# Attention and feed-forward kernel: first query halves on two hardware queues ahead of the other keys, first bursts on the first half, score pieces in unit pairs

## Chip, cores, metric

One core of one Trainium2 chip. The metric is device time in microseconds, the median of several executions. Runs are told apart by state (fast or slow); all timed runs below are fast ones. The one single run, of the experiment with delayed software loads, has the state unknown, and only its trace is used.

## The reference

Grouped-query attention (8 batches, 16 query heads, 4 key heads, 384 positions, 64 elements per head), then a feed-forward layer with a squared ReLU:

```python
scores = (1/sqrt(64)) * q @ k.T          # per batch and head; 4 query heads share a key head
attn   = softmax(scores)
x      = (attn @ v) -> [3072, 1024]
out    = (max(x @ w_in, 0) ** 2) @ w_out # w_in 1024x2048, w_out 2048x1024
```

## The kernel before

A recorder collects operations with what they read and write, and turns them into semaphore waits. It also keeps a clock per engine with a cost for each operation. A loop, the list scheduler, uses these clocks to choose what TensorE does next. The loads of batch 0, with the key of head 0 (`k0`) first:

```python
def first_loads():
    for g0, g1 in ((0, 1), (1, HKV)):              # k0, then the other keys: both on sync
        R.add("sync", lambda e, ...: e.dma_start(k_f32[...g0:g1...], k[0, g0:g1]...),
              writes=[("k_f32", g) ...], dma=f"kf{g0}", cost=0.4 if g1 == 1 else 1.6, issue=0.4)
    for n in range(2):                             # the two q halves of key head 0: both on scalar
        R.add("scalar", lambda e, n=n: e.dma_start(q_f32[:, 2*n:2*n+2, :], q[0, 2*n:2*n+2]...),
              writes=[("q_f32", n)], dma=f"qf{n}", cost=0.8, issue=0.4)
# ... cut: GpSimd's own (software) loads and casts, in its program order:
load_q(0, 4, 8); ...; load_v(0); load_q(0, 8, 12); load_q(0, 12, 16); load_w_in(0)
dup_k(0, 1, 2)        # cast of key head 1, waits for the other keys
load_k(1); dup_k(0, 2, 4); aug_v(0, "gpsimd"); load_q(1, 0, 8); ...
```

Batch 0 is scored in small bursts. Each burst is two or four matmuls, and one exponential on ScalarE reads its result. A unit is one key head's block of 128 keys; units 0 to 2 belong to head 0. Elements 0 to 383 of a unit's row need the first q half, the rest the second.

```python
for group in ((0,), (1, 2), (3, 4), (5, 6), (7,), (8, 9), (10, 11)):
    if len(group) == 2 and group[1] < NU - 1:
        smalls += [[(u, 0, 512)] for u in group] + [[(u, 512, 256) for u in group]]
    else:
        smalls += [[(u, c0, 384)] for c0 in (0, 384) for u in group]
turn_q = [(0, 0, "a"), (0, 0, "c")]   # transposes of the first and second q half
turn_q += [(b, g, w) for b in range(2) for g in range(HKV) for w in "kq" if (b, g) != (0, 0)]
# ... cut: in the scheduling loop
if turn_q and (b == 0 or pairs < 6 or x_done[0] == 8):
    cand.append((..., 3.5 * b + 1, "turn"))        # priority 1; a score burst of batch 0 has 0
```

The softmax here doesn't subtract the row's maximum and nothing guards it: scores larger than these inputs give would overflow.

## Time and profile before

| | |
|---|---|
| median | 430.89 us (3 runs, 430.09 to 431.02) |
| span of the profiled run | 428.1 us |
| TensorE busy | 423.2 us, 99% |
| ScalarE busy | 194.9 us, 46% |
| half-clock window in the profile | 8.08 to 11.49 us |

TensorE has 99% of the span, and the chain of waits is TensorE's for 98%. Only what delays TensorE's start can be removed without removing work. The prediction shows the lines. Here is the trace's transfer view of the kernel before from 3.8 to 5.0 us. Its columns are the queue row, the packets, the megabytes moved, and the time those packets took as a share of 16 engines' time. Row q1 is the sync queue, q10 the scalar queue, q0 GpSimd's software loads.

```profile
DMA packets 565, 0.32 MB, mean 266 GB/s; under 512 B 270, under 2 KB 565, under 8 KB 565
q0 software_dynamic: 242, 0.09, 67.6%
q10 hardware_dynamic: 233, 0.17, 41.6%
q1 hardware_dynamic: 90, 0.06, 15.2%
```

### The profile page before, as it was taken

What the parts mean: (1) busy time and instruction counts of PE and PEld (TensorE: products, weight loads), DVE (VectorE), ACT (ScalarE), POOL (GpSimd) and SP (SyncE); (2) the same over time, 40 slices, a digit from 0 to 9 for tenths busy, and PEclk for the clock granted to TensorE, in tenths of its full rate; (3) what the DMA queues carried; (4) which work ended last, traced back from release to release, by engine and by line L of the source; (5) the groups of instructions that cost most, each with busy time, mean ns of one, the idle gap of its engine ahead of it and who ended that gap; (6) DMA issues with size and microseconds to landing.
All of it is one profiled execution on the core that took longest, in us unless ns stands there. A gap on an engine that the chain in (4) does not pass through costs nothing.

```text
span 428.1 us, 7844 instructions
## 1 busy us (share of the span) xinstructions
PE 423.2 (99%) x3467; PEld 232.2 (54%) x3467; DVE 158.8 (37%) x334; ACT 194.9 (46%) x194; POOL 55.1 (13%) x67
## 2 busy tenths in 40 slices
PE   7999999999999999999999999999999999999997
PEld 5565554565445654456554465645564465446544
DVE  2674432254223542325432253523342144214412
ACT  6947740557545675446765459550230033003300
POOL 8680011413040022004000000000000000000000
PEclk8999999999999999999999999999999999999999
DMA  9999999999599179369647410032001100110012
GB/s 180 193 198 204 187 195 190 236 152 130 90 188 166 20 133 141 98 145 145 64 80 140 89 45 18 16 92 81 37 2 49 73 26 2 49 73 26 1 66 83
DMA packets 95347, 43.90 MB, mean 103 GB/s; under 512 B 75728, under 2 KB 89296, under 8 KB 95312
## 3 DMA queue, kind: packets, MB, share of 16 engines
q0 software_dynamic: 36544, 17.44, 32.4%
q1 hardware_dynamic: 58224, 25.57, 28.0%
q8 instruction: 27, 0.44, 0.4%
q10 hardware_dynamic: 544, 0.39, 0.3%
q14 instruction: 8, 0.07, 0.1%
HBM read 35.65 MB, written 12.58 MB: 113 GB/s over the span
## 4 chain that ended last, share of the span: by engine, by line
PE 98%; DMA 1%; ACT 0%; DVE 0%; ACTq 0%; issue 0%
PE ps L431 40%; PE ps L480 39%; PE ps L374 9%; PE ps L349 7%; PE ps L328 1%; DMA q_f<-in_q_dram 1%; PE ps L302 1%; PE ps L407 0%; PE ps L286 0%; ACT expT L338 0%; DVE o_sb L389 0%; ACT q_st L551 0%; ACTq L218 0%; DVE y_sb L489 0%; DVE rinv L383 0%
## 5 line engine op out<-in xcount | busy, mean ns | idle before, releaser
L431 PE MATMUL ps<-xT,w_in_sb 128*128 128x384 bf16 x1024 | 175.0, 326 | 0.0
L480 PE MATMUL ps<-w_out_sb,h2T 128*128 128x512 bf16 (+2 forms) x784 | 172.0, 375 | 0.0
L359 ACT ACTIVATE expT<-ps 128x3072 bf16<-128x3072 f32 x42 | 114.4, 2725 | 57.7 <-PE ps L349 57.1
L431 PEld LDWEIGHTS ps<-xT,w_in_sb 128*128 128x128 bf16 x1024 | 96.8, 98 | 69.2 <-issue 6.4
L441 ACT ACTIVATE h2T<-hr 128x384 bf16<-128x384 f32 x128 | 64.3, 520 | 148.8 <-DVE hr L439 148.7
L480 PEld LDWEIGHTS ps<-w_out_sb,h2T 128*128 128x128 bf16 x784 | 73.8, 98 | 87.6 <-issue 5.4
L439 DVE TENSOR_SCALAR hr<-ps 128x384 f32<-128x384 f32 x128 | 71.1, 557 | 104.8 <-PE ps L431 104.8
L489 DVE COPY y_sb<-ps 128x512 f32<-128x512 f32 (+2 forms) x49 | 33.4, 681 | 127.4 <-PE ps L480 127.4
L374 PEld LDWEIGHTS ps<-v_aug,expT 128*128 128x128 bf16 x1152 | 39.8, 97 | 6.6 <-DVE o_sb L389 0.7
L374 PE MATMUL ps<-v_aug,expT 128*128 128x65 bf16 x1152 | 41.6, 193 | 0.1
L389 DVE TENSOR_TENSOR o_sb<-ps,rinv 128x384 bf16<-128x384 f32 x64 | 35.7, 558 | 2.2
L349 PE MATMUL ps<-qT,kT 64*128 64x512 bf16 (+1 forms) x336 | 34.6, 325 | 0.0
L349 PEld LDWEIGHTS ps<-qT,kT 64*128 64x128 bf16 x336 | 13.0, 94 | 20.7 <-issue 5.4
L383 DVE RECIPROCAL rinv<-ps 128x6 f32<-128x6 f32 x64 | 12.2, 190 | 24.1 <-PE ps L374 24.0
L338 ACT ACTIVATE expT<-ps 128x1024 bf16<-128x1024 f32 (+1 forms) x20 | 17.2, 941 | 1.7 <-PE ps L328 1.5
L263 POOL COPY v_aug<-v_st 128x768 bf16<-128x768 bf16 x8 | 6.7, 832 | 87.0 <-PE ps L374 71.9
L258 POOL COPY k_dup<-k_st 128x1536 bf16<-128x1536 bf16 x7 | 10.3, 1467 | 36.7 <-DMA k_st<-in_k_dram 36.7
L231 POOL DMA_DIRECT2D q_st<-in_q_dram x17 | 14.9, 888 | 0.9 <-POOLq L726 0.8
L205 POOL DMA_DIRECT2D k_st<-in_k_dram x7 | 5.3, 762 | 39.6 <-DMA qT<-q_st 39.6
L328 PE MATMUL ps<-qT,kT 64*128 64x384 bf16 (+2 forms) x48 | 8.0, 360 | 0.3 <-DVE qT L309 0.2
L241 POOL DMA_DIRECT2D w_in_sb<-in_moe_w_in_dram x8 | 7.1, 897 | 0.0
L224 POOL DMA_DIRECT2D v_st<-in_v_dram x8 | 6.3, 792 | 0.1
(26 smaller groups left out, 44.5 us busy)
## 6 DMA issues: line engine op xcount, KB each, us to landing
out_dram<-y_sb SPq DMA_DIRECT2D x47, 256.0 KB, 2.0
q_st<-in_q_dram POOLq DMA_DIRECT2D x14, 384.0 KB, 9.1
w_in_sb<-in_moe_w_in_dram POOLq DMA_DIRECT2D x8, 512.0 KB, 12.1
w_out_sb<-in_moe_w_out_dram POOLq DMA_DIRECT2D x4, 1024.0 KB, 27.0
v_st<-in_v_dram POOLq DMA_DIRECT2D x8, 192.0 KB, 10.6
k_st<-in_k_dram POOLq DMA_DIRECT2D x7, 192.0 KB, 4.3
q_st<-in_q_dram POOLq DMA_DIRECT2D x3, 192.0 KB, 5.2
xT<-o_sb SPq DMA_TRANSPOSE x28, 4.3
```

The lines of the kernel that those rows point to most:

```text
L231: R.add("gpsimd", lambda g: g.dma_start(q_st[st][:, h0:h1, :], q[b, h0:h1].rearrange("h (p j) d -> p h (j d)", j=NJ)), writes=[("q_st", st ...
L328: mm = pe.matmul(ps[:, base + x, m * wide:(m + 1) * wide], kT[b % 2][64 * x:64 * x + 64, u, :], q_cols(b, u // NJ, x, c0, c0 + wide))
L338: R.add("scalar", lambda e: e.activation(dst, src, AF.Exp, scale=0.125), reads=keys, writes=[("expT", (b * NU + u) % NEX, t) for u, _, _ i ...
L349: m = pe.matmul(flat[:, k0 * HC + c0:k0 * HC + c1], kT[b % 2][64 * x:64 * x + 64, u + k0, :], q_cols(b, (u + k0) // NJ, x, c0, c1))
L359: R.add("scalar", lambda e: e.activation(dst, src, AF.Exp, scale=0.125), reads=keys, writes=[("expT", (n + m) % NEX, t) for m in range(2) ...
L374: m = pe.matmul(po[:, f - 6 * s2, 0:D + 1], w, v_aug[b % 2][:, g * NJ + j, 0:D + 1], start=(j == 0), stop=(j == NJ - 1))
L389: R.add("vector", lambda e: e.tensor_tensor(dst, srcv, rbv, ALU.mult), reads=[("bank", i), ("rinv", r)], writes=[("o_sb", o, s2)], cost=0.48)
L431: m = pe.matmul(bank(i)[:, 0:S], w_in_sb[:, kc, c * 128:(c + 1) * 128], xT[b % NXT][:, kc, :], start=(kc == 0), stop=(kc == NKC - 1))
L439: R.add("vector", lambda e: e.tensor_scalar_max(hr[r][:, :], bank(i)[:, 0:S], 0.0), reads=[("bank", i)], writes=[("hr", r)], cost=0.48)
L441: R.add("scalar", lambda e: e.activation(h2T[b % 2][:, c, :], hr[r][:, :], AF.Square), reads=[("hr", r)], writes=[("h2T", b % 2, c)], cost ...
L480: m = pe.matmul(bank(i)[:, 0:n], h2T[b % 2][:, c, i3 * 128:(i3 + 1) * 128], w_out_sb[:, c, c0:c1], start=(c == 0), stop=(c == NFC - 1))
L489: R.add("vector", lambda e: e.tensor_copy(ysl, bank(i)[:, 0:n]), reads=[("bank", i)], writes=[("y", yb)], cost=0.08 + n / 960)
```

## The change

The intent is to have TensorE score as soon as the first q half is there. The second q half moves from the scalar to the sync queue, ahead of the other keys. The second half's transposes may not stand ahead of the first burst. The bursts are grouped so that the first two need the first q half alone.

```diff
-        for g0, g1 in ((0, 1), (1, HKV)):
-            R.add("sync", lambda e, g0=g0, g1=g1: e.dma_start(
+        def keys(g0, g1):
+            R.add("sync", lambda e: e.dma_start(
   ...
-                ..., cost=0.4 if g1 == 1 else 1.6, issue=0.4)
-        for n in range(2):
-            R.add("scalar", lambda e, n=n: e.dma_start(
+                ..., cost=0.4 if g1 == 1 else 1.1, issue=0.4)
+        def queries(n, eng):
+            R.add(eng, lambda e: e.dma_start(
   ...
+        keys(0, 1)
+        queries(0, "scalar")
+        queries(1, "sync")
+        keys(1, HKV)
   ...
-    for group in ((0,), (1, 2), (3, 4), (5, 6), (7,), (8, 9), (10, 11)):
-        if len(group) == 2 and group[1] < NU - 1:
+    for group in ((0, 1), (2, 3), (4, 5), (6, 7), (8, 9), (10, 11)):
+        if 0 < group[0] < NU - 2:
   ...
-        if turn_q and (b == 0 or pairs < 6 or x_done[0] == 8):
+        if turn_q and (b == 0 or pairs < 6 or x_done[0] == 8) and (sc_q[0] != (0, 0) or w in "ka"):
```

More of the change, by code (lines that the diff above doesn't have):

```diff
@@ L210, in first_loads @@
     def first_loads():
-        for g0, g1 in ((0, 1), (1, HKV)):
-            R.add("sync", lambda e, g0=g0, g1=g1: e.dma_start(
+        def keys(g0, g1):
+            R.add("sync", lambda e: e.dma_start(
                 k_f32[:, g0 * NJ:g1 * NJ, :].rearrange("p (g j) d -> p g (j d)", j=NJ),
                 k[0, g0:g1].rearrange("g (p j) d -> p g (j d)", j=NJ)),
-                writes=[("k_f32", g) for g in range(g0, g1)], dma=f"kf{g0}", cost=0.4 if g1 == 1 else 1.6, issue=0.4)
-        for n in range(2):
-            R.add("scalar", lambda e, n=n: e.dma_start(
+                writes=[("k_f32", g) for g in range(g0, g1)], dma=f"kf{g0}", cost=0.4 if g1 == 1 else 1.1, issue=0.4)
+        def queries(n, eng):
+            R.add(eng, lambda e: e.dma_start(
                 q_f32[:, 2 * n:2 * n + 2, :], q[0, 2 * n:2 * n + 2].rearrange("h (p j) d -> p h (j d)", j=NJ)),
                 writes=[("q_f32", n)], dma=f"qf{n}", cost=0.8, issue=0.4)
+        keys(0, 1)
+        queries(0, "scalar")
+        queries(1, "sync")
+        keys(1, HKV)
     def load_v(b):
```

## The prediction

> **What bounds the kernel now.** I read the page first. The busy line and the chain that ended last say that TensorE is the bound almost from end to end:
>
> ```profile
> span 428.1 us, 7844 instructions
> PE 423.2 (99%) x3467; PEld 232.2 (54%) x3467; DVE 158.8 (37%) x334; ACT 194.9 (46%) x194; POOL 55.1 (13%) x67
> PE 98%; DMA 1%; ACT 0%; DVE 0%; ACTq 0%; issue 0%
> ```
>
> The reader is to see how little is not TensorE: 2% of 428.1 us is some 8 us. The change touches only the first loads and the scores of batch 0, so all it can remove is part of that. I then asked the trace for the chain of waits in its first 31 us, to see where those microseconds lie:
>
> ```profile
> 0.73 0.46 ACTq L218
> 1.23 4.05 DMA q_f<-in_q_dram
> 5.30 0.52 ACT q_st L551
> 5.82 0.14 issue
> 5.96 0.33 PE ps L302 x3
> 6.29 0.29 PE ps L328 x2
> 6.59 0.82 ACT expT L338
> 7.46 0.39 PE ps L328 x2
> 7.85 0.52 PE ps L302 x6
> ```
>
> (Columns: start, duration, what.) The head of the program hangs on the second q load: it is issued at 1.23 us and lands at 5.28, ScalarE casts it (L551), TensorE transposes it (L302), the first score burst (L328) follows, its exponential (L338) frees the banks, and from 7.46 us on every piece of the chain is TensorE, apart from 0.9 us near 23 us. So before 7.46 us lies the removable time.
>
> The timeline of that stretch shows why the first score burst waited for the second q load though it reads only the first half:
>
> ```profile
> 4.96 0.36 DVE L309 COPY qT<-ps 128x384 bf16<-128x384 bf16 x1 [0.38 <-PE ps L302]
> 5.30 0.51 ACT L551 CAST q_st<-q_f 128x384 bf16<-128x384 f32 x1 [0.97 <-DMA q_f<-in_q_dram]
> 5.96 0.33 PE L302 MATMUL ps<-ident,q_st 128*128 128x128 bf16 x3 [1.03 <-ACT q_st L551]
> 6.22 0.34 PE L328 MATMUL ps<-qT,kT 64*128 64x384 bf16 x2
> 6.32 0.36 DVE L309 COPY qT<-ps 128x384 bf16<-128x384 bf16 x1 [1.00 <-PE ps L302]
> 6.59 4.35 ACT L338 ACTIVATE expT<-ps 128x768 bf16<-128x768 f32 x5 [0.78 <-PE ps L328]
> 11.54 7.03 ACT L338 ACTIVATE expT<-ps 128x1024 bf16<-128x1024 f32 x8 [0.59 <-PE ps L328]
> 18.72 5.91 ACT L338 ACTIVATE expT<-ps 128x1024 bf16<-128x1024 f32 x7 [0.16 <-PE ps L328]
> ```
>
> The transposed first half is ready at 4.96 + 0.36 = 5.32 us. But TensorE runs in program order, and the transposes of the second half stand ahead of the burst: TensorE idles 1.03 us for the cast, transposes, and only then scores. The last three lines show the second thing: from 6.59 to 24.63 us ScalarE has only 0.59 + 0.16 us of idle time, so the 20 exponentials of batch 0 and TensorE run neck and neck there. No transfer holds TensorE up after 6 us: in the list of waits of the TensorE rows over the whole span, none names a DMA.
>
> **What the Trainium skill says.** Four places bear on this.
> - "DMA: Bandwidth & Descriptors", section "Issuing engines are not separate DMA queues": transfers from SP, ACT and GpSimd share the same 16 engines, and issuing from several saves only issue time. The trace agrees: from 3.2 to 3.8 us the two hardware rows together moved 355 GB/s, and from 5.0 us, when the software row has the engines, it is about 180 GB/s. So moving a load to the other queue buys no bandwidth; only its order can matter.
> - Same page, "Queues, rings and completion order": each engine takes turns between rows packet by packet. The trace agrees only in part: from 2.2 to 3.2 us row q10 moved 0.19 MB and q1 0.10, from 3.2 to 3.8 us q1 0.17 and q10 0.04, from 3.8 to 4.4 us q10 0.14 and q1 0.06. That is rather one transfer after the other in order of issue. I reckon with that order.
> - "TensorE: Matmul & The Clock Gate", "What's actually happening": the array runs at half rate until a free-running window of 3413 ns was busy, and falls back after an idle one. The trace agrees: the granted clock is 1.00 until about 8.1 us, 0.50 until 11.5, then 1.00, so one such window after the sparse stretch from 4.7 to 8.1 us.
> - "ScalarE: Activation LUTs", "What ACT_TABLE_LOAD costs": an activation with immediate scale costs 186 ns + 0.833 ns per element. That gives 826 ns for 768 and 1039 for 1024; the groups by form show 816 and 1025 ns. So the new grouping, if it keeps the counts, keeps ScalarE's total.
>
> **The change part by part.**
>
> *Loads.* The bytes stay: one key group 96 KB, two q halves of 192 KB, the other keys 288 KB. Issue order was k0 and q-first (both 0.73 us), other keys (about 1.13), q-second (1.23). Now q-second is second on the sync queue, ahead of the other keys. In order of issue it takes the place that the other keys had: they had moved about 0.23 MB by 3.8 us (row q1's 0.33 MB less k0's 0.10). The 0.20 MB of q-second should be through at about 3.7 us. The first q half had moved by 3.2 us and landed at 3.8, so 0.6 us for the completion: q-second lands at about 4.3 us instead of 5.28, an estimate. ScalarE casts the first half from 3.82 to 4.33, so the second cast follows at 4.35 to 4.9 us instead of 5.30 to 5.81. The other keys come last: at 4.4 us 0.76 of the 0.79 MB had moved before, and the total is the same, so they land at about 5.3 us instead of 5.1. GpSimd casts them at 6.09 us without having waited, after issuing four software loads, so it loses nothing.
>
> *First bursts.* The new condition lets the first burst go before the second half's transposes, and with units (0, 1) as the first group two bursts in a row read only the first half. Burst 0 starts when the first half's copy is done: 5.32 + 0.05 us (the second burst began 0.05 us after its copy ended at 6.68) = 5.37 instead of 6.21. Its exponential starts 0.38 us later, as before (6.59 - 6.21): 5.75 instead of 6.59, so 0.84 us sooner. The first half itself (land, cast, transpose, copy) doesn't move, so it is the new head. The second half's transposes come behind burst 1, at about 5.9 us; their copy is done at about 6.7, and the exponential of burst 1 runs until 5.75 + 2 x 0.82 = 7.4, so burst 2 isn't late for ScalarE.
>
> *Grouping.* Counted from the loops: before 2 + 3 + 3 + 3 + 2 + 3 + 4 = 20 bursts, now 4 + 4 x 3 + 4 = 20; eight of 768 elements and twelve of 1024 in both. No instruction and no time is added on ScalarE or TensorE. What moves: the pair (2, 3) straddles two key heads, so the second context piece of the first head becomes possible after the seventh burst instead of the fifth.
>
> *What reaches the end.* ScalarE's chain moves by 0.84 us. TensorE's chain moves by less. At 7.46 us it had, inside the wait for the first exponential, also done the transposes of key head 1 (0.27 us at the pace of its later rows). Their input is GpSimd's cast, 6.09 + 0.55 = 6.64 us, which doesn't move; so they now stand behind burst 2 and cost 0.27 us on the path. 0.84 - 0.27 = 0.57 us if TensorE is the narrower of the two, 0.84 if ScalarE is. Middle 0.7 us. From there on the work is fixed and TensorE is full, so what is won at the head stays won: nothing later waits for a load. The weights for the first up-projection piece were issued at 5.21 us, took 7.1 us and are first read at 15.1, so at 14.3 they are there still.
>
> 430.89 - 0.7 = 430.2 us; with a small chance for the clock (below), 430.1.
>
> **The rivals.**
> 1. *The clock swallows or doubles it.* Two bursts move into the idle gap of the window from 4.7 to 8.1 us. If that makes it busy enough, the half-rate window goes; TensorE would save up to 3.4 x 0.5 = 1.7 us there, but ScalarE's idle time in it is only 0.59 us, so about 0.6 more: 429.6. Against it: TensorE's busy time in that window is only some 2.2 us of 3.4 and rises little. The window is free-running, so it may fall differently in each run anyway. I give it one in four, worth 0.15 us on average.
> 2. *The transfers are what counts, and the gain is hidden.* If rows shared evenly, q-second would still be early, but q-first could be late because a second q transfer runs beside it; each 0.1 us it lands later is 0.1 us lost. Or the other keys land past 6.1 us because the software loads take half the engines; then GpSimd stalls, and its later loads with it. For it speaks the drop to 180 GB/s at 4.5 us; against it 0.8 us of slack. Then 430.5 to 430.9.
> 3. *The order shuffles.* The program order of TensorE comes from a list scheduler with its own cost table; a head that is earlier can change the order of transposes, context pieces and up-projection pieces until about 28 us. The straddling pair gives TensorE less filler early. That can cost or save some 0.3 us: 429.8 to 430.8.
> 4. *More than the head.* If ScalarE is the true bound until 24.6 us and its 0.59 us pause goes too, 429.5.
>
> **Range and chances.** The three runs before spread from 430.09 to 431.02, as wide as the gain; that and the rivals give 429.1 to 431.0 for 8 in 10. Two per cent is 8.6 us, more than all the time in which TensorE isn't the chain, so faster by that much is next to excluded; slower would need a new stall of 8 us in a later stage, which only a badly reshuffled order could make. Faster 0.01, same 0.98, slower 0.01.
>
> **What would show it.** In the changed profile: the second q cast right behind the first, at about 4.4 us; the first L328 burst at about 5.4 and the first exponential at about 5.75 us, two bursts of 64x384 ahead of the second group of L302 transposes; the last exponential of batch 0 some 0.6 to 0.85 us before 24.63; the keys cast by GpSimd still at about 6.1 us without a wait; the span about 427.4 us. Wrong would be: the first cast later than 3.82 us, GpSimd waiting for the keys, a TensorE wait in 6 to 28 us that eats the lead, or a half-clock window that is gone or doubled.

## The result, and the profile after

| | before | after |
|---|---|---|
| median of 6 runs | 430.49 us (429.81 to 431.07) | 431.63 us (431.40 to 432.19) |
| span of the profiled run | 428.1 us | 429.9 us |
| first score burst of batch 1 in that run | 30.60 us | 32.32 us |

The ratio is 1.0029, with a 95% interval of 1.0015 to 1.0042. A ratio here is the mean time of one kernel's fast runs over that of the other's in the same rounds, so it is not quite the ratio of the medians. The kernel got slightly slower, where 0.8 us less was predicted. The class is right (within 2%); the sign and the range are not.

The page of the changed kernel: its span, its chain by engine, and the chain by line:

```profile
span 429.9 us, 7817 instructions
PE 97%; DMA 1%; issue 0%; ACT 0%; SPq 0%; POOL 0%; DVE 0%
PE ps L437 39%; PE ps L486 39%; PE ps L380 8%; PE ps L355 7%; PE ps L334 1%; DMA k_f<-in_k_dram 1%; PE ps L308 1%; PE ps L292 1%; ACT expT L344 0%; PE ps L413 0%; POOL k_dup L264 0%; SPq L219 0%; SPq L213 0%; DVE y_sb L495 0%
```

The transfer on the chain was that of q before, and is that of the keys now. The chain of the changed kernel in order of time (start, duration, what):

```profile
1.20 0.41 SPq L219
1.61 0.05 issue
1.66 5.75 DMA k_f<-in_k_dram
7.41 0.05 issue
7.47 0.51 POOL k_dup L264
7.98 0.05 issue
8.03 0.50 PE ps L292 x3
8.53 0.43 PE ps L334
```

The other keys are issued third on the sync queue at 1.66 us and land at 7.41 us. The prediction had put them at 5.3 us, with need for them only at 6.09. GpSimd's cast, and the transposes of key head 1 behind it (L292), start only then. The timeline of the changed kernel shows the rest:

```profile
3.99 1.05 ACT L557 CAST q_st<-q_f 128x384 bf16<-128x384 f32 x2 [0.19 <-DMA q_f<-in_q_dram]
5.35 0.50 PE L334 MATMUL ps<-qT,kT 64*128 64x384 bf16 x4 [0.45 <-DVE qT L315]
5.73 1.51 ACT L344 ACTIVATE expT<-ps 128x768 bf16<-128x768 f32 x2 [0.69 <-PE ps L334]
7.47 0.50 POOL L264 CAST k_dup<-k_f 128x384 bf16<-128x384 f32 x1 [1.34 <-DMA k_f<-in_k_dram]
8.03 0.50 PE L292 MATMUL ps<-ident,k_dup 128*128 128x128 bf16 x3 [1.91 <-POOL k_dup L264]
8.46 0.50 PE L334 MATMUL ps<-qT,kT 64*128 64x384 bf16 x2
9.01 0.81 ACT L344 ACTIVATE expT<-ps 128x768 bf16<-128x768 f32 x1 [1.77 <-PE ps L334]
14.81 11.17 ACT L344 ACTIVATE expT<-ps 128x1024 bf16<-128x1024 f32 x13 [0.58 <-PE ps L334]
```

The first three lines are what the change wanted: both q casts back to back, the first bursts at 5.35 us, the first exponential at 5.73. Then TensorE waits 1.91 us for the keys. The burst at 8.46 us needs only head 0 and the second q half, which was copied at 6.16 + 0.36 = 6.52 us. It is late because the transposes of key head 1 stand ahead of it in TensorE's order. ScalarE has a hole of 1.77 us there, and its last exponential of batch 0 ends at 14.81 + 11.17 = 25.98 us, where it was 24.63.

The transfer view of the changed kernel from 3.8 to 5.0 us answers to that shown of before:

```profile
DMA packets 341, 0.17 MB, mean 143 GB/s; under 512 B 227, under 2 KB 341, under 8 KB 341
q0 software_dynamic: 222, 0.08, 69.6%
q1 hardware_dynamic: 119, 0.09, 29.2%
```

The scalar row is empty. All rows together move half of what they moved before. The software row's share is nearly that of before (69.6%, 67.6%); what differs is when it comes in. From 3.8 to 4.4 us it has 12.8% before and 67.8% after, and the hardware rows move 0.20 MB before and 0.03 MB after. A byte of the software row takes about 2.5 times as much packet time as one of the sync row (69.6% for 222 packets of 0.38 KB on average, 29.2% for 119 of 0.74 KB). Packet time is not the engines' own time, for packets overlap: alone on the engines, from 5.0 to 6.0 us of the kernel before, the software row's packets add up to 154.8%. By 4.4 us the hardware rows had moved about 0.51 MB (summed over windows of the trace), against 0.76 MB before; the keys are the missing part.

After about 32 us the two kernels run the same course. The first burst of batch 1 is 1.72 us late, a burst near 280 us (278.18 before, 279.91 after) 1.73 us, and the spans differ by 1.73 us. So all of the loss of this pair of runs arises in the head. (The profiled pair lies further apart than the medians, which differ by 1.14 us.)

### The profile page after: what moved, and what is told of

Its sections match the earlier page's. It is cut to its first block, busy times and chain, and to the rows that moved or that the text cites. A ratio compares the mean times of both kernels' runs of the same rounds, so it can differ in the third digit from the quotient of the medians.

```text
span 429.9 us, 7817 instructions
## 1 busy us (share of the span) xinstructions
PE 422.1 (98%) x3440; PEld 232.7 (54%) x3467; DVE 158.7 (37%) x334; ACT 195.1 (45%) x194; POOL 55.1 (13%) x67
## 4 chain that ended last, share of the span: by engine, by line
PE 97%; DMA 1%; issue 0%; ACT 0%; SPq 0%; POOL 0%; DVE 0%
PE ps L437 39%; PE ps L486 39%; PE ps L380 8%; PE ps L355 7%; PE ps L334 1%; DMA k_f<-in_k_dram 1%; PE ps L308 1%; PE ps L292 1%; ACT expT L344 0%; PE ps L413 0%; POOL k_dup L264 0%; SPq L219 0%; SPq L213 0%; DVE y_sb L495 0%
## 5 line engine op out<-in xcount | busy, mean ns | idle before, releaser
L486 PE MATMUL ps<-w_out_sb,h2T 128*128 128x512 bf16 (+2 forms) x757 | 167.6, 375 | 1.6 <-issue 0.3
```

What stands on the lines that cost most here:

```text
L486: m = pe.matmul(bank(i)[:, 0:n], h2T[b % 2][:, c, i3 * 128:(i3 + 1) * 128], w_out_sb[:, c, c0:c1], start=(c == 0), stop=(c == NFC - 1))
```

## The experiments

The theory, A: the loss is the late landing of the other keys. It comes from their place as third load in one hardware row, and it costs time through GpSimd's cast and TensorE's program order. The rival, B: the new order of bursts, the unit pairs, or the clock cost the time. TensorE's order could be compared instruction by instruction between versions, so "the same order" below is a fact of the programs.

The first four ran on one chip, beside 11 runs of the kernel before (median 430.04 us). The next four ran on another, beside 11 runs of before (median 430.03).

### Two loads in each row

```diff
-        keys(1, HKV)              # third on sync
+        keys(1, HKV, "scalar")    # second on scalar, behind the first q half
```

> The changed kernel, with the other keys issued from the scalar queue behind the first q half, so that each hardware row carries two loads; TensorE's and VectorE's program order is instruction for instruction that of the changed kernel. Theory A (the loss is the late landing of the other keys, 7.41 us, because three loads stand in one row and the third meets the software loads): the keys land by about 5.6 us, GpSimd's first key cast starts at 6.1 us without a wait, the exponentials run without the 1.77 us hole, and the time is 429.8 us, ratio to before 0.998. Rival B (the loss is in the new order of bursts and pairs, or in the clock): the keys may land early, but the time stays at 431.4 to 431.8 us, ratio 1.002 to 1.003.

429.46 us median, ratio 0.9979 (0.9961 to 0.9997). The timeline:

```profile
5.69 4.09 ACT L344 ACTIVATE expT<-ps 128x768 bf16<-128x768 f32 x5 [0.66 <-PE ps L334]
9.93 13.00 ACT L344 ACTIVATE expT<-ps 128x1024 bf16<-128x1024 f32 x15
6.10 0.55 POOL L264 CAST k_dup<-k_f 128x384 bf16<-128x384 f32 x1
6.70 0.34 PE L292 MATMUL ps<-ident,k_dup 128*128 128x128 bf16 x3 [0.61 <-POOL k_dup L264]
```

and its transfers from 3.8 to 5.0 us:

```profile
DMA packets 516, 0.31 MB, mean 261 GB/s; under 512 B 191, under 2 KB 516, under 8 KB 516
q10 hardware_dynamic: 326, 0.24, 59.4%
q0 software_dynamic: 166, 0.06, 55.6%
q1 hardware_dynamic: 24, 0.01, 3.2%
```

TensorE's order is that of the changed kernel, entry for entry, and so is the rest but for the row of one load. GpSimd casts at 6.10 us without a wait, and 20 exponentials run from 5.69 to 22.93 us almost without a hole. Rival B is out for the new order and the pairs; the clock comes up again below. Theory A holds, in that the keys' late landing is the loss. This run doesn't show why they were late: the edit also lets them be issued 0.43 us sooner (1.23 us, not 1.66), and no run separates the row from that. The profiled run is one of the two quickest of its six (428.62 us) and has no half-clock window at all, so its timeline is a favourable one.

### The old loads with the new order

The loads of before, with the burst condition and the pairs of the change.

> The loads of the kernel before with the burst condition and the unit pairs of the changed kernel; TensorE's order is that of the changed kernel. Theory A: first burst at about 5.4 us and first exponential at 5.75 us as in the changed kernel, keys at 5.1 us, second q half at 5.28 us, no hole; 429.8 us, ratio 0.998: the whole predicted gain without the new loads. Rival B (order and pairs cost the time): 431.4 to 431.8 us.

429.34 us median (429.24 to 429.38), ratio 0.9981 (0.9966 to 0.9997). TensorE's order is again entry for entry that of the changed kernel. So the new order is worth about 0.8 us (0.0019 of 430) with no change of loads at all. In detail the expectation missed: the profiled run has its first burst at 5.62 and first exponential at 6.17 us, later than 5.75, because the array ran at half clock there (three transposes at 6.38 us took 0.50 us, against 0.34 us at 5.75 us in the version with two loads per row).

### The new loads with the old order

> The new loads alone, with the burst condition and the groups of the kernel before. Theory A: keys land at 7.4 us as in the changed kernel, TensorE stands before the transposes of key head 1 until about 8 us, the time is 431.3 to 432 us, ratio 1.002 to 1.004. Rival B: the second q half is early and nothing else changed, 430.0 to 430.4 us.

432.32 us, ratio 1.0053 (1.0035 to 1.0071), as theory A expects, and slightly more. Its GpSimd line, after a landing later than in the first profile:

```profile
8.29 0.50 POOL L264 CAST k_dup<-k_f 128x384 bf16<-128x384 f32 x1 [2.16 <-DMA k_f<-in_k_dram]
8.85 0.50 PE L292 MATMUL ps<-ident,k_dup 128*128 128x128 bf16 x3 [2.53 <-POOL k_dup L264]
```

The three runs together separate the two parts: the new loads cost, the new order gains.

### The true landing time told to the scheduler

```diff
-  cost=0.4 if g1 == 1 else 1.1
+  cost=0.4 if g1 == 1 else 3.3
```

> The changed kernel with one number changed: the list scheduler's cost for the other keys' load is 3.3 instead of 1.1, which puts its landing at the 7.4 us that the trace showed. The loads are untouched. The scheduler now puts score bursts 2 and 3 ahead of the transposes of key head 1, where the changed kernel has those transposes first. Theory A1 (the late keys hurt because the program order makes TensorE wait for them while bursts that need only key head 0 are ready): keys still at 7.4 us, but exponentials of bursts 2 and 3 follow burst 1 without a hole, the time falls to 430.0 to 430.5 us. Theory A2 (late keys hurt whatever the order is): 431 to 432 us. Rival B (new order as such): unclear, near 431.5.

432.41 us, ratio 1.0052: the expectation missed. The run doesn't decide its question, for two reasons. The exponentials of bursts 2 and 3 did follow without the hole, and the first burst of batch 1 started at 31.73 us, 0.6 us sooner than in the first profile of the changed kernel. But the other number in the scheduler's clocks reshuffled the whole program, and a later batch got a new wait of TensorE:

```profile
PE ps L355 <- DMA qT<-q_st: 1.3, 1, 1.3
```

(Columns: who waited for whom, us in total, times, longest.) No other version's waits of TensorE after 30 us name a DMA. So the question was asked again without that side effect.

### Only the order of key head 1's transposes

```diff
   if turn_q and (...) and (sc_q[0] != (0, 0) or w in "ka") \
+          and ((b, g, w) != (0, 1, "k") or sc_q[0][1] >= 4):
```

The changed kernel with its own loads and costs; these transposes come behind the first four bursts. TensorE's order differs only in entries 8 to 21 (the expectation had reckoned with the changed kernel's order from entry 15 on).

> The changed kernel with its loads and its cost table, only with the transposes of key head 1 held back in TensorE's order until the four score bursts of the first pair are out; from the fifteenth entry of TensorE's order on it is the changed kernel's again, so the later wait of the run with the true cost (1.3 us for the transpose of a later batch's q) can't come back. Theory A1 (in-order blocking carries a good part of the loss): bursts 2 and 3 and their exponentials follow without a hole, the first burst of batch 1 starts 0.5 to 0.8 us sooner than in the changed kernel, 430.9 to 431.3 us. Theory A2 (the late keys delay GpSimd and all key heads, and the work behind them is the same): within 0.3 us of the changed kernel.

430.67 us, ratio 1.0011 (0.9997 to 1.0026), a little better than expected. The changed kernel was run again beside it:

> The changed kernel itself, for a comparison on the same chip as the next three. Theory: 431.4 to 432.3 us, other keys landing between 7.4 and 8.2 us.

431.69 us, ratio 1.0039 (1.0024 to 1.0054). So about 1.0 us of the loss is the in-order wait in front of bursts that were ready, with whatever the clock adds to it. The two profiles differ like this; first the changed kernel's second profile, in which the keys landed still later, at 8.66 us:

```profile
1.66 7.00 DMA k_f<-in_k_dram
8.72 0.51 POOL k_dup L264
9.28 0.50 PE ps L292 x3
```

The timeline of the version with the order changed:

```profile
6.14 1.51 ACT L344 ACTIVATE expT<-ps 128x768 bf16<-128x768 f32 x2 [1.18 <-PE ps L334]
7.84 1.51 ACT L344 ACTIVATE expT<-ps 128x768 bf16<-128x768 f32 x2 [0.20 <-PE ps L334]
8.65 0.50 PE L292 MATMUL ps<-ident,k_dup 128*128 128x128 bf16 x3 [0.44 <-POOL k_dup L264]
10.37 2.00 ACT L344 ACTIVATE expT<-ps 128x1024 bf16<-128x1024 f32 x2 [1.02 <-PE ps L334]
```

Four exponentials are out before 9.4 us, and TensorE waits 0.44 us for the keys, not 3.29 as in the changed kernel's run beside it. The rest of the loss stays, as the keys are still late (landing at 8.04 us) and the later heads with them.

### Software loads held back until the keys are there

```diff
-    load_q(0, 4, 8)
+    load_q(0, 4, 8, [("k_f32", 1)])    # GpSimd's first load waits for the other keys
```

> The changed kernel, but GpSimd's first software load waits until the other keys have landed, so nothing of the software row runs beside them. Read for the landing time of the other keys alone; the total will be worse, as all software loads start some 4 us later. Theory S (the keys are late because the software loads share the engines with them once the other hardware row is empty): they land at 5.0 to 5.5 us, as the prediction said. Rival R (the third load of a row is slow by itself, its transfers made late): 6.5 us or later still.

434.33 us against 430.26 for before, and, as announced, the total says nothing. The landing does:

```profile
1.66 3.81 DMA k_f<-in_k_dram
```

and so does the transfer view from 3.8 to 5.0 us:

```profile
q1 hardware_dynamic: 385, 0.28, 75.8%
```

Issued at the same 1.66 us, and third in the same row, the keys land at 5.46 us when no software load runs beside them. The sync row moves 0.28 MB in these 1.2 us, against 0.09. So the third place alone doesn't make the load slow; the software loads beside it do. In the five profiles with the changed loads and the software loads as they were (two of the changed kernel, and the three versions above that keep its loads) the landing was between 7.41 and 8.66 us.

Still open is why the software row starts earlier there. Its first packets come at 3.2 to 3.5 us wherever the scalar row holds one load, and at 4.0 to 4.3 us wherever it holds two, though its first load is issued at the same 1.23 us. That is seen in every profile of the two kinds. The run with the software loads held back gives a measure: there the first software load is issued at 5.76 us, with the hardware rows all but done, and its first packet comes at 7.35 us, 1.6 us later. After 1.23 us that delay is 2.0 to 2.2 us with one load in the scalar row and 2.8 to 3.0 us with two. So it is rather two loads in each row that hold the software row back than three and one that bring it forward. The cause isn't tested.

### Dummy matmuls in TensorE's pauses

```diff
   turn_q_pe(b, g, spare, ...)
+  if w in "ac":
+      warm_up(dict(a=4, c=6)[w], 0.0)     # 4 and 6 dummy 128x128 matmuls
```

on top of two loads in each row. Without them that version's six times fall into 428.37 and 428.62, and 429.38 to 429.70.

> The version with two loads in each hardware row, plus 4 and 6 dummy 128x128 matmuls in TensorE's two pauses (before the first score burst and before the transposes of key head 1); all else in TensorE's order is the same. Theory C (the 1 us between the fast and the slower of its six times, 428.4 to 428.6 against 429.4 to 429.7, is a half-clock window that comes when the array was too idle before): all times near 428.5 us. Rival: the dummies delay the path or the clock isn't it, 429.4 us or more.

428.69 us median (428.42 to 429.13), ratio 0.9968 (0.9954 to 0.9981): the best version. Apart from the two entries of dummies TensorE's order is unchanged, and ScalarE's exponentials run in one piece:

```profile
6.19 16.79 ACT L344 ACTIVATE expT<-ps 128x768 bf16<-128x768 f32 x20 [1.06 <-PE ps L334]
```

The start isn't sooner (the first exponential at 6.19 us; the array was still at half clock, as the four score matmuls before it took 0.82 us and not 0.50), but the group of slower times is gone. That fits theory C, that part of the spread is a half-clock window after a sparse stretch. It isn't shown: no slower run of the version without dummies was profiled. The two versions ran on different chips, so the 0.8 us between their medians is not a direct comparison; the ratios to before (0.9968 and 0.9979) have overlapping intervals.

### Without the unit pairs

Two loads in each row and the burst condition, with the old groups.

> The version with two loads in each hardware row, with the groups of the kernel before ((0), (1, 2), ...) in place of the unit pairs; the burst condition stays. If the second burst on the first half alone matters: exponential 1 waits for the second q half's transposes and copy, so some 0.2 to 0.5 us slower than the 429.5 us with the pairs. If only the first burst matters: 429.5 us.

429.40 us, ratio 0.9985 (0.9968 to 1.0002). Against 0.9979 with pairs, the intervals overlap almost wholly: inconclusive. The trace shows the expected wait of the second exponential (0.25 us), but also a wait of 0.9 us for a software q load, and both kernels have bimodal times.

## Why the prediction was wrong

*Right.* The bound, and the removable time at the head. The first burst at 5.37 us (measured 5.35) and the first exponential at 5.75 (5.73). The second q cast right behind the first (both in one piece from 3.99 us). No cost from the grouping on ScalarE. The rigid carry of the head's balance to the end: 1.72 us at 32 us, 1.73 at the end. Where the keys are in time, a gain of the predicted 0.7 us is there: 0.0021 and 0.0019 of 430 us are 0.9 and 0.8 us. How far it comes in the predicted way is less sure. With the old loads the profiled run had its first exponential at 6.17 us, only 0.42 us sooner than before and not 0.84, and with two loads in each row the profile has no half-clock window. The two estimates for an exponential, 826 and 1039 ns, were within 2% of the 816 and 1025 measured before.

One thing was right by slack. The first q half was later, as the second rival feared: it was cast at 3.99 us and not at 3.82, which the prediction had named as a sign of being wrong. Its transposes still started at 4.55 us (4.52 before), so the first burst was on time.

*The step that failed* is in the part on loads: "at 4.4 us 0.76 of the 0.79 MB had moved before, and the total is the same, so they land at about 5.3 us instead of 5.1. GpSimd casts them at 6.09 us without having waited, after issuing four software loads, so it loses nothing." The hardware rows had moved 0.51 MB by then, not 0.76, and the keys landed at 7.41 us (8.66 in a second profile). I took the hardware loads' progress from the kernel before and only exchanged their places. But with one row holding three loads and the other one, the software row was under way some 0.8 us earlier, and the third load ran beside it. The two rates from which the prediction concluded that only the order of a load can matter, 355 and 180 GB/s, had not tested that: with two loads in each row the keys were still the last load, and landed at 5.30 us. The run with the software loads held back gives 5.46 us for the same load in the same place, close to what the prediction reckoned.

*The second failed step* follows from it: the transposes of key head 1 "now stand behind burst 2 and cost 0.27 us on the path". They stand ahead of burst 2: with its cost of 1.1 for the keys' load the scheduler counted on the keys by then, and with 3.3 it put the bursts first. TensorE waited 1.91 us for the keys with two bursts ready. Moving these transposes behind the bursts took 431.69 to 430.67 us.

*The rivals.* The second one named this cause, and even its witness, the drop to 180 GB/s. It was sized wrongly, at 430.5 to 430.9 us, because it was set against 0.8 us of slack computed from the failed landing. The first rival had the clock lose its half-rate window in one case of four; in both profiles of the changed kernel the window was twice as long instead (7.63 to 14.46 us and 7.52 to 14.34, against 8.08 to 11.49 before). The wait for the keys had left the array idle ahead of it; that this is the cause, and how much of the loss it makes, no run isolates. The fourth rival, that ScalarE's 0.59 us pause goes as well, is what the version with two loads in each row shows; but as its half-clock window is gone too, that profile doesn't tell the fourth rival from the first.

## What to carry to other kernels

When a load is moved ahead of another, reckon the landing of the one that is now last from what will run beside it then, not from what ran beside it before. Here the same load in the same place landed at 5.46 us without the software loads, and at 7.41 to 8.66 us beside them. And check which program order rests on an assumed landing time: here TensorE's wait for late data held back work that was ready, and that was about 1.0 us of the 1.7 us by which the changed kernel lay above the kernel before. Measured from the version with the new order and the old loads (429.34 us, on another chip) the loss is some 2.4 us, and 1.0 is less than half of that.

## What the Trainium skill lacked or had wrong

- "DMA: Bandwidth & Descriptors", section "Issuing engines are not separate DMA queues", says that issuing on several engines only saves the sequencer's issue time. Here the same loads spread two and two over the hardware rows instead of three and one took the time from a ratio of 1.0029 to 1.0039 down to 0.9979, with the other keys' cast at 6.10 us and not at 7.47. The issue itself took 0.4 to 0.5 us per load, and the keys were issued 0.43 us sooner; they landed at 5.30 us and not at 7.41. That the engines are shared agrees with the runs. The page lacks that the software row came in later wherever both hardware rows held two loads (4.0 to 4.3 us, not 3.2 to 3.5).
- The same page, "Queues, rings and completion order", says that rows are taken in turn, packet by packet. The section gives no share of time for rows with unequal packets. Here the software row's packets took 69.6% for 0.08 MB beside a hardware row with 29.2% for 0.09 MB. Those packets were about half as large (0.38 KB and 0.74 KB); how much of the difference that makes, no run here separates.
- "TensorE: Matmul & The Clock Gate", "What's actually happening": the 3.4 us windows agree (3.41 us before, 6.83 us, two of them, after). The page warns that clock events in a profile can be unreliable. It doesn't say that the granted clock can be blank before its first recorded change: the run of the old loads with the new order is listed with a clock of 1.0, though its first record is at 9.55 us and three transposes before it took 0.50 us, as in half-clock windows, and not 0.34.
